# GpSimd's arithmetic in the tiles of an attention and two-layer expert kernel goes to VectorE, its copies of shared halves to ScalarE

## The chip, the cores and the metric

The kernel runs on one core of a Trainium2 chip. That core has a matrix engine (TensorE, in the profile PE, with its weight loads as PEld), three engines for elementwise work (VectorE or DVE, ScalarE or ACT, GpSimd or POOL) and SyncE (SP), which issues most of the DMAs. Each engine works through its own queue in order. The metric is the device time of one execution in microseconds (us), and the time before is the median of three runs. All engines read and write the on-chip SBUF; TensorE writes its results to PSUM, which VectorE and ScalarE read as well.

## The reference

Four steps follow one another, all in float32:

```python
p_packed = sm_attn(p, k, v)            # 8 batches x 8 heads, 32 packed rows over 576 keys
out = sm_attn(q, p_packed, p_packed)   # 576 queries over the 32 packed rows
x = out as (4608, 512)                 # tokens x model
h = x @ w_in                           # 512 -> 2048
g = where(h >= 1, h, where(h <= -1, 0, (h + 1)**2 / 4))
x = g @ w_out                          # 2048 -> 512
# experts: the gate picks one of 8 for each token
logits = x @ w_gate; e = argmax; gate = softmax(logits)[e]
y = gate * (relu(x @ w1[e]) @ w2[e])   # 512 -> 1024 -> 512
```

`sm_attn` is softmax attention with a scale of 1/8. The second attention's softmax runs over 32 columns only.

## The kernel before

**High and low parts.** The matmuls run in a reduced float32 form. A product of two float32 operands is made of three matmuls: high by high, high by low and low by high. So each operand is split: ScalarE rounds it to its high part (a copy into the reduced type), and another engine subtracts that from the original, which gives the low part (names that end in `l`: `al`, `gl`, `xl`).

**Stages.** Packing (to about 102 us by the trace, with some of it going on behind the first tile) makes the first attention, prepares the weights of the first layer, and multiplies them with the packed rows. Then come twelve tiles of tokens with the first two layers. From 820 us on the expert slots follow: 18 of 256 tokens each and a tail of half slots, with the weights of one expert loaded and split for each.

**Tiles.** A pair of batches has 1152 tokens and is cut into three tiles: A (320 columns), M (512) and B (320). B starts where M ends, and A ends where M starts; but the last 64 columns of A make up one block of 128 for the second matmul together with B, so A passes on 256 columns and keeps 64, and B passes on 384. The order of the twelve is M A B, A B M, A B M, M A B. Each tile has 16 steps, one for each 128 of the 2048 hidden columns. In one step `ffn1` makes `h` in PSUM (6 matmuls per batch in the tile, L718), `hidden` makes `g` of it, and `tile_y` adds the step before to `y` in PSUM with three matmuls per block of 128 tokens (L723, L724 with the high part, L725 with the low part).

**`hidden`, the chain of a step.** ScalarE: Relu of 0.5 h + 0.5 (L740) and its square (L741); VectorE: max and min with h (L742), the last reader of `h`; ScalarE: the high part `gh` (L747); then the low part `gl` (L748), on GpSimd in A tiles and on VectorE in M and B tiles. GpSimd also copies A's last 64 columns to `kept` (L750) and, in a B tile, from there to the front of `rt` (L739). `h` has two banks of PSUM, and `gh`, `gl` and `rt` two buffers each.

**Beside it**, in `bg`, steps of other work are laid out by hand for each step: the second attention for the next tile, in chains of three pieces for 256 or 320 columns (`score`, `expo`, `back`; A and B tiles take two chains of 320, M tiles four of 256); the router of the tile before (`gate_items`: eight dot products for each block of 128 tokens, L547, then the places in the expert lists and an indirect DMA by GpSimd, L594); and in the third tile of a pair and the step after it the weights' product with the next packed rows (L361 to L366).

**Order.** SyncE's queue is in the order of the program. For the other engines a planner writes the order: it takes the program's order as priorities and runs through it with costs of its own for each instruction, so a change of engine can change the order of others as well.

Of the kernel before, what the change touches and what calls it, by code (L numbers as in the profile page):

```python
# [15 lines left out]
ALU = mybir.AluOpType  # L16
# [7 lines left out]
P = 128  # L24
TW = 512
HB = 64
# [22 lines left out]
SPLIT = 256  # L49


def tile_kind(t):


    p, m = divmod(t, 3)
    return ("MAB", "ABM", "ABM", "MAB")[p][m]
# [6 lines left out]
def tile_width(t):  # L63
    return TW if tile_kind(t) == "M" else SPLIT + HB
# [13 lines left out]
def tile_blocks(t):  # L78


    return {"A": [0, P], "B": [0, P, 2 * P], "M": [0, P, 2 * P, 3 * P]}[tile_kind(t)]
# [3 lines left out]
def attn_moe_kernel(ctx, tc, qT, kT, vv, pT, wcat, wg, w2cat, out):  # L85
    nc = tc.nc
    ctx.enter_context(tc.manual_schedule(engines={nc.sync.engine}))
    pe, act, dve, pool, sp = nc.tensor, nc.scalar, nc.vector, nc.gpsimd, nc.sync

    def f32(ap):  # L90
        return ap.bitcast(F32)
# [108 lines left out]
    def ps_tile(name):  # L200
        if not done:
            return y_tile(name)
        return a_tile([P, 512], name)
# [25 lines left out]
    def attn_chain(col0, b, ws, n, g, ah, al, pl, sfx):  # L229


        st = {}
        nb = n // 32

        def load():
            qr = pl.tile([P, 2, SPLIT + HB], F32, name="qr" + sfx, tag="qr", bufs=2)
            (act if done else sp).dma_start(qr[:, :, :n], qT[b, 2 * g:2 * g + 2, :, ws:ws + n].rearrange("q p s -> p q s"))
            st["qr"] = qr

            st["sT"], st["aT"] = qr[:, 0, :n].rearrange("p (a r) -> p a r", r=32), qr[:, 1, :n]  # L240

        def score():
            ps = ps_tile("s2" + sfx)
            for q in range(2):
                s = q ^ (b % 2)
                r = slice(D * s, D * s + D)
                pe.matmul(ps[r, :n], lhsT=pkf[:, 2 * g + q, r], rhs=st["qr"][:, q, :n], start=True, stop=True)
            sT = st["sT"]
            dve.transpose(out=sT, in_=ps[:, :n].rearrange("p (a r) -> p a r", r=32))
            mx = pl.tile([P, (SPLIT + HB) // 32, 1], F32, name="mx" + sfx, tag="mx")  # L250
            dve.tensor_reduce(out=mx[:, :nb, 0], in_=sT, axis=AX.X, op=ALU.max)
            pool.tensor_tensor(out=sT, in0=sT, in1=mx[:, :nb, :].to_broadcast([P, nb, 32]), op=ALU.subtract)

        def expo():
            sT = st["sT"]
            act.activation(sT, sT, AF.Exp, scale=SCALE)
            sm = pl.tile([P, (SPLIT + HB) // 32, 1], F32, name="sm" + sfx, tag="sm")
            dve.tensor_reduce(out=sm[:, :nb, 0], in_=sT, axis=AX.X, op=ALU.add)
            dve.tensor_scalar(out=sm[:, :nb, 0], in0=sm[:, :nb, 0], scalar1=1e-9, scalar2=None, op0=ALU.add)
            dve.reciprocal(sm[:, :nb, 0], sm[:, :nb, 0])  # L260
            pool.tensor_tensor(out=sT, in0=sT, in1=sm[:, :nb, :].to_broadcast([P, nb, 32]), op=ALU.mult)

        def back():
            aT = st["aT"]
            hi, lo = ah[:, g, col0:col0 + n], al[:, g, col0:col0 + n]
            dve.transpose(out=aT.rearrange("p (a r) -> p a r", r=32), in_=st["sT"])
            act.copy(hi, aT)
            pool.tensor_tensor(out=lo, in0=aT, in1=f32(hi), op=ALU.subtract)

        return load, [score, expo, back]  # L270

    x_tiles = {}
# [11 lines left out]
    def wtile(n, shape, dt, name):  # L284

        return wpool.tile(shape, dt, name=name, tag=n)
# [440 lines left out]
    kept = []  # L727

    def hidden(t, fc, ps):

        k = tile_kind(t)
        W = tile_width(t)
        gh = work.tile([P, TW], F32R, name=f"gh{FC * t + fc}", tag="gh", bufs=2)
        gl = work.tile([P, TW], F32R, name=f"gl{FC * t + fc}", tag="gl", bufs=2)
        vk = work.tile([P, TW], F32, name=f"rt{FC * t + fc}", tag="rt", bufs=2)
        v, n = vk[:, :W], W
        if k == "B":
            v, n = vk[:, HB:HB + W], HB + W
            pool.tensor_copy(vk[:, :HB], kept[0][:, fc])  # L739
        act.activation(v, ps[:, :W], AF.Relu, bias=half, scale=0.5)  # L740
        act.activation(v, v, AF.Square)  # L741
        dve.scalar_tensor_tensor(out=v, in0=ps[:, :W], scalar=1.0, in1=v, op0=ALU.max, op1=ALU.min)  # L742
        if k == "A":
            n = SPLIT
            if fc == 0:
                kept[:] = [wtile("ws0", [P, FC, HB], F32, f"kept{t}")]
        act.copy(gh[:, :n], vk[:, :n])  # L747
        (pool if k == "A" else dve).tensor_tensor(out=gl[:, :n], in0=vk[:, :n], in1=f32(gh[:, :n]), op=ALU.subtract)  # L748
        if k == "A":
            pool.tensor_copy(kept[0][:, fc], v[:, SPLIT:])  # L750
        return [(gh[:, c:c + P], gl[:, c:c + P]) for c in tile_blocks(t)]

    y_tiles = {}
# [258 lines left out]
    def step():  # L1012
        t, fc = divmod(len(done), FC)
        if fc == 0:
            schedule_tile(t)
        G = t * FC + fc
        ps = h_tile(G, f"h{t}_{fc}")
        ffn1(t, fc, ps)
        gs = hidden(t, fc, ps)
        if done:  # L1020
            tile_y(*done[-1])
        done.append((t, fc, gs))
        for fn in bg.pop(G, []):
            fn()
# [87 lines left out]
```

## Time and profile before

| | |
|---|---|
| median of 3 runs | 1249.33 us (1248.11 to 1250.98) |
| the profiled execution | 1249.28 us, of which the span is 1247.3 |
| TensorE busy | 1193.9 us (96%) |
| its weight loads | 995.3 us (80%) |
| VectorE busy | 944.6 us (76%) |
| ScalarE busy | 730.0 us (59%) |
| GpSimd busy | 325.5 us (26%) |
| mean granted clock of TensorE | 0.984 of full speed |

The span runs from the first instruction to the last one's end. Busy is the time in which an engine runs at least one instruction, and instructions on one engine can overlap at their ends. The ends of matmuls are modelled, so a TensorE that is called busy can still be short of its peak. A wait is idle time of an engine ahead of an instruction, and it is put down to what ended it.

### The profile page before, as it was taken

To read this page: it belongs to the slowest core of one execution; us is meant where nothing else is said; L and a number is where in the kernel's file an instruction comes from. 1 tells how busy PE (TensorE), PEld (TensorE's weight loads), DVE (VectorE), ACT (ScalarE), POOL (GpSimd) and SP (SyncE) were. 2 spreads that over 40 slices of the span, in tenths; PEclk is the share of its full clock that TensorE was granted. 3 is DMA by queue.
4 is the path that set the end of the run, shared out by engine and by line. 5 is a ranking of instruction groups with operands and counts; after the bars stand their busy time and mean duration, and the time that the engine had idled before them with its cause. 6 is when DMAs were issued, how large, how long until landed. Compare 5 with 4: busy or idle time off the path is not lost. (4 is left out here: it accounts for less than half of the span.)

```text
span 1247.3 us, 21251 instructions
## 1 busy us (share of the span) xinstructions
PE 1193.9 (96%) x7234; PEld 995.3 (80%) x7234; DVE 944.6 (76%) x2222; ACT 730.0 (59%) x1430; POOL 325.5 (26%) x567
## 2 busy tenths in 40 slices
PE   5787999999999999999999999999999999999997
PEld 2455888778778887678888887788999999999996
DVE  8888867988895959977869679899766666666663
ACT  4666656667566556565565455655565555555653
POOL 3221116623741105731211265512101000010010
PEclk8988999999999999999999999999999999999999
DMA  9995780143211232111331000601212512111150
GB/s 347 370 328 176 283 245 22 43 142 126 68 47 62 68 113 101 50 44 35 108 126 45 28 18 35 186 18 50 78 36 68 170 44 60 35 54 49 34 178 21
DMA packets 70179, 128.18 MB, mean 103 GB/s; under 512 B 10281, under 2 KB 46633, under 8 KB 66864
## 3 DMA queue, kind: packets, MB, share of 16 engines
q1 hardware_dynamic: 56464, 97.33, 24.2%
q0 software_dynamic: 5840, 18.95, 4.1%
q10 hardware_dynamic: 7760, 10.49, 2.7%
q8 instruction: 59, 0.97, 0.3%
q14 instruction: 56, 0.46, 0.1%
HBM read 162.31 MB, written 31.77 MB: 156 GB/s over the span
## 5 line engine op out<-in xcount | busy, mean ns | idle before, releaser
L718 PE MATMUL h<-ah,pw 128*128 128x256 f32 (+1 forms) x1024 | 242.6, 302 | 8.2 <-DVE rt L742 8.0
L869 DVE TENSOR_TENSOR sw<-raw,sw 128x1024 fp32r<-128x1024 f32 (+1 forms) x152 | 180.9, 1209 | 77.9 <-ACT sw L867 77.8
L885 PEld LDWEIGHTS gh<-gx,sw 128*128 128x128 f32 x1728 | 227.1, 191 | 12.8
L885 PE MATMUL gh<-gx,sw 128*128 128x256 f32 x1728 | 230.5, 283 | 0.0
L723 PE MATMUL y<-wo,gh 128*128 128x512 f32 x576 | 229.9, 399 | 0.6 <-ACT kp L423 0.6
L724 PE MATMUL y<-wo,gh 128*128 128x512 f32 x576 | 228.5, 397 | 0.0
L547 DVE CUSTOM_DVE_ANT_0 jk<-yr,wgb 128x512 bf16<-128x512 f32 x288 | 219.1, 761 | 5.6 <-ACT yr L775 3.5
L718 PEld LDWEIGHTS h<-ah,pw 128*128 128x128 f32 x1024 | 176.5, 190 | 31.0 <-DVE rt L742 13.4
L867 ACT CAST sw<-raw 128x1024 fp32r<-128x1024 f32 (+1 forms) x160 | 156.5, 1004 | 59.1 <-PE gy L725 53.9
L725 PE MATMUL y<-wo,gl 128*128 128x512 f32 x576 | 186.3, 400 | 2.1 <-POOL gl L748 1.9
L740 ACT ACTIVATE rt<-h,half 128x320 f32<-128x320 f32 (+1 forms) x192 | 111.0, 580 | 102.6 <-PE h L718 86.2
L747 ACT CAST gh<-rt 128x512 fp32r<-128x512 f32 (+2 forms) x192 | 98.1, 512 | 96.6 <-DVE rt L742 59.1
L718 PE MATMUL h<-al,pw 128*128 128x256 f32 (+1 forms) x512 | 152.7, 298 | 0.0
L742 DVE SCALAR_TENSOR_TENSOR rt<-h,rt 128x320 f32<-128x320 f32 (+1 forms) x192 | 105.5, 551 | 51.1 <-ACT rt L741 46.3
L908 POOL DMA_INDIRECT out<-go,xm x37 | 36.8, 993 | 362.3 <-ACT go L907 303.1
L725 PEld LDWEIGHTS y<-wo,gl 128*128 128x128 f32 x576 | 105.8, 189 | 30.0 <-POOL gl L748 5.1
L723 PEld LDWEIGHTS y<-wo,gh 128*128 128x128 f32 x576 | 108.7, 189 | 23.3 <-issue 2.1
L724 PEld LDWEIGHTS y<-wo,gh 128*128 128x128 f32 x576 | 108.9, 189 | 18.7
L889 ACT ACTIVATE ggh<-gh 128x256 fp32r<-128x256 f32 x144 | 55.0, 382 | 109.5 <-PE gh L885 103.8
L724 PE MATMUL gy<-sw,ggh 128*128 128x512 f32 x288 | 113.9, 395 | 0.0
L723 PE MATMUL gy<-sw,ggh 128*128 128x512 f32 x288 | 113.8, 395 | 0.0
L748 DVE TENSOR_TENSOR gl<-rt,gh 128x512 fp32r<-128x512 f32 (+1 forms) x128 | 84.1, 658 | 25.3 <-ACT gh L747 21.2
(220 smaller groups left out, 1762.5 us busy)
## 6 DMA issues: line engine op xcount, KB each, us to landing
raw<-in_w2cat SPq DMA_DIRECT2D x76, 1024.0 KB
ws<-wsd SPq DMA_DIRECT2D x48, 512.0 KB
wr<-in_wcat SPq DMA_DIRECT2D x16, 1024.0 KB
kp<-in_kT SPq DMA_DIRECT2D x16, 576.0 KB
xb<-xs SPq DMA_DIRECT2D x72, 128.0 KB
vr<-in_vv SPq DMA_DIRECT2D x16, 512.0 KB
wsd<-ws SPq DMA_DIRECT2D x8, 1024.0 KB
qr<-in_qT ACTq DMA_DIRECT2D x16, 320.0 KB
```

Of the source, the lines that this page charges most:

```text
L547: dve.tensor_tensor_reduce(out=junk, in0=rows[j][:, :DM], in1=wgb[0][:, e, :], scale=1.0, scalar=0.0, op0=ALU.mult, op1=ALU.add, accum_out ...
L718: pe.matmul(ps[:, col0:col0 + n], lhsT=w[:, g, part, c], rhs=x[:, g, col0:col0 + n], start=(n_mm == 0), stop=(n_mm == 5))
L723: pe.matmul(y, lhsT=gh, rhs=wh, start=first, stop=False)
L724: pe.matmul(y, lhsT=gh, rhs=wl, start=False, stop=False)
L725: pe.matmul(y, lhsT=gl, rhs=wh, start=False, stop=last)
L740: act.activation(v, ps[:, :W], AF.Relu, bias=half, scale=0.5)
L742: dve.scalar_tensor_tensor(out=v, in0=ps[:, :W], scalar=1.0, in1=v, op0=ALU.max, op1=ALU.min)
L747: act.copy(gh[:, :n], vk[:, :n])
L748: (pool if k == "A" else dve).tensor_tensor(out=gl[:, :n], in0=vk[:, :n], in1=f32(gh[:, :n]), op=ALU.subtract)
L867: act.copy(w[:, n, 0], r)
L869: (pool if sid == 0 and i else dve).tensor_tensor(out=w[:, n, 1], in0=r, in1=f32(w[:, n, 0]), op=ALU.subtract)
L885: pe.matmul(ps[:, :SL], lhsT=first(sid, 4 * (fc // 4) + k, part)[:, c], rhs=rh[:, k, :], start=(n_mm == 0), stop=(n_mm == 3 * KD - 1))
```

## The change

Six instructions get another engine; operands, sizes and places in the program stay. The subtraction of the maximum and the multiplication with the reciprocal sum in the second attention, and the low part of its result, go from GpSimd to VectorE, in all tiles. So does the low part of `hidden` in A tiles, which makes all tiles alike. The two copies of 64 columns (`kept`) go from GpSimd to ScalarE. On GpSimd stay the indirect DMAs, the router's running counts (L571 to L573), copies of token numbers (L593), copies in the packing (L395), and eight low parts of the first slot's weights (L869).

```diff
 def attn_chain / score:
-    pool.tensor_tensor(out=sT, in0=sT, in1=mx[:, :nb, :].to_broadcast([P, nb, 32]), op=ALU.subtract)
+    dve.tensor_tensor(out=sT, in0=sT, in1=mx[:, :nb, :].to_broadcast([P, nb, 32]), op=ALU.subtract)
 expo:
-    pool.tensor_tensor(out=sT, in0=sT, in1=sm[:, :nb, :].to_broadcast([P, nb, 32]), op=ALU.mult)
+    dve.tensor_tensor(out=sT, in0=sT, in1=sm[:, :nb, :].to_broadcast([P, nb, 32]), op=ALU.mult)
 back:
-    pool.tensor_tensor(out=lo, in0=aT, in1=f32(hi), op=ALU.subtract)
+    dve.tensor_tensor(out=lo, in0=aT, in1=f32(hi), op=ALU.subtract)
 def hidden:
     if k == "B":
-        pool.tensor_copy(vk[:, :HB], kept[0][:, fc])
+        act.copy(vk[:, :HB], kept[0][:, fc])
...
     act.copy(gh[:, :n], vk[:, :n])
-    (pool if k == "A" else dve).tensor_tensor(out=gl[:, :n], in0=vk[:, :n], in1=f32(gh[:, :n]), op=ALU.subtract)
+    dve.tensor_tensor(out=gl[:, :n], in0=vk[:, :n], in1=f32(gh[:, :n]), op=ALU.subtract)
     if k == "A":
-        pool.tensor_copy(kept[0][:, fc], v[:, SPLIT:])
+        act.copy(kept[0][:, fc], v[:, SPLIT:])
```

## Rows read from the trace of the kernel before

**Rows 1.** Busy us by stage: length, then PE, PEld, DVE, ACT, POOL, clock, DMA share, GB/s.

```profile
40.00:102.10 62.10, 47.45 (x472) 28.14 (x476) 52.02 (x101) 37.35 (x92) 16.05 (x26) 0.84 0.98 348
...
191.10:235.20 44.10, 43.82 (x228) 35.18 (x227) 39.62 (x126) 27.58 (x77) 31.94 (x46) 1.00 0.09 28
235.20:290.80 55.60, 54.99 (x276) 45.55 (x275) 47.61 (x124) 39.68 (x92) 16.42 (x34) 1.00 0.41 133
290.80:341.00 50.20, 48.80 (x245) 38.19 (x244) 42.28 (x122) 30.20 (x70) 32.01 (x50) 1.00 0.23 77
...
468.80:516.20 47.40, 45.98 (x233) 36.25 (x232) 44.97 (x118) 29.67 (x69) 31.28 (x47) 1.00 0.23 79
...
721.00:764.00 43.00, 41.37 (x211) 33.91 (x210) 37.40 (x106) 24.35 (x57) 28.87 (x44) 1.00 0.05 19
...
820.20:1247.30 427.10, 419.56 (x2634) 376.86 (x2632) 284.64 (x512) 234.04 (x350) 41.81 (x44) 1.00 0.22 64
```

**Rows 2.** Waits of TensorE, 191 to 820 us: total us, times, longest.

```profile
PE h L718 <- DVE rt L742: 8.0, 9, 2.0
PE y L725 <- POOL gl L748: 1.9, 4, 1.1
...
PEld h L718 <- DVE rt L742: 13.2, 15, 2.3
PEld y L725 <- POOL gl L748: 5.1, 7, 1.5
```

**Rows 3.** The dots by line in four A tiles, then an M tile: busy us, mean ns.

```profile
L547 DVE CUSTOM_DVE_ANT_0 jk<-yr,wgb 128x512 bf16<-128x512 f32 x32 | 25.0, 780 | 1.5 <-ACT yr L775 1.1
...
L547 DVE CUSTOM_DVE_ANT_0 jk<-yr,wgb 128x512 bf16<-128x512 f32 x24 | 19.6, 817 | 0.2
...
L547 DVE CUSTOM_DVE_ANT_0 jk<-yr,wgb 128x512 bf16<-128x512 f32 x29 | 26.5, 915 | 0.1
...
L547 DVE CUSTOM_DVE_ANT_0 jk<-yr,wgb 128x512 bf16<-128x512 f32 x32 | 26.8, 839 | 2.5 <-ACT yr L775 2.3
...
L547 DVE CUSTOM_DVE_ANT_0 jk<-yr,wgb 128x512 bf16<-128x512 f32 x24 | 16.3, 681 | 0.4 <-ACT yr L775 0.2
```

**Rows 4.** Timeline in two A tiles: start us, us, instruction, count.

```profile
200.23 0.88 DVE L742 SCALAR_TENSOR_TENSOR rt<-h,rt 128x320 f32<-128x320 f32 x2
...
483.36 1.25 DVE L547 CUSTOM_DVE_ANT_0 jk<-yr,wgb 128x512 bf16<-128x512 f32 x1
...
482.80 2.42 POOL L748 TENSOR_TENSOR gl<-rt,gh 128x256 fp32r<-128x256 f32 x2
```

**Rows 5.** GpSimd by line over the span: busy us, mean ns, idle before.

```profile
L748 POOL TENSOR_TENSOR gl<-rt,gh 128x256 fp32r<-128x256 f32 x64 | 59.6, 932 | 12.2 <-ACT gh L747 4.9 <-PE y L725 4.7 <-DMA qr<-in_qT 1.3
...
L750 POOL COPY kept<-rt 128x64 f32<-128x64 f32 x64 | 32.2, 503 | 42.6 <-DVE rt L742 39.7 <-PE h L718 2.5
L268 POOL TENSOR_TENSOR al<-qr,ah 128x256 fp32r<-128x256 f32 (+1 forms) x32 | 31.8, 993 | 41.1 <-ACT ah L267 41.0
L252 POOL TENSOR_TENSOR qr<-qr,mx 128x256 f32<-128x256 f32 (+1 forms) x32 | 26.0, 812 | 132.8 <-issue 52.4 <-DVE mx L251 45.9 <-PE h L718 33.5
L261 POOL TENSOR_TENSOR qr<-qr,sm 128x256 f32<-128x256 f32 (+1 forms) x32 | 25.9, 808 | 35.2 <-DVE sm L260 26.4 <-DVE rs L424 3.6 <-ACT rt L741 2.9
L739 POOL COPY rt<-kept 128x64 f32<-128x64 f32 x64 | 23.8, 375 | 68.5 <-DVE gl L748 67.5 <-DVE pk L219 0.5 <-issue 0.2
```

**Rows 6.** VectorE by line and shape over the span.

```profile
L742 DVE SCALAR_TENSOR_TENSOR rt<-h,rt 128x320 f32<-128x320 f32 x128 | 61.7, 484 | 17.2 <-ACT rt L741 15.6 <-POOL yr L593 0.4
L890 DVE SCALAR_TENSOR_TENSOR ggl<-gh,ggh 128x256 fp32r<-128x256 f32 x144 | 59.9, 416 | 49.5 <-ACT ggh L889 47.0 <-PE y L725 2.4
```

**Rows 7.** Waits of ScalarE and VectorE, 191 to 820 us.

```profile
ACT rt L740 <- POOL gl L748: 7.5, 10, 2.4
...
DVE gl L748 <- ACT gh L747: 15.8, 26, 1.9
```

**Rows 8.** ScalarE by line and shape over the span.

```profile
L218 ACT CAST pk<-bt 64x64 fp32r<-64x64 f32 x64 | 13.1, 205 | 2.5 <-PE bt L209 1.8
```

## The prediction

> **What bounds the kernel now.** I read the busy times by stage first, one stage for each of the twelve tiles. A tile's stretch runs from its first Relu (L740) to the next tile's. From 820 us on, the expert slots run with TensorE busy 419.6 of 427.1 us, and no line that the change touches runs there [rows 1]. The gain or loss has to arise before 820 us. There, the B tile at 235 us has TensorE busy 55.0 of 55.6 us. The four A tiles (191, 291, 469 and 721 us) stand out for something else: GpSimd is busy 29 to 32 us of 43 to 50, against 16 in that B tile and 16 in the last 62 us of the packing. VectorE is busy 39.62 + 42.28 + 44.97 + 37.40 = 164.3 of their 184.7 us, 89%, so 20.4 us idle in all [rows 1]. In A tiles two engines are nearly full, TensorE and VectorE, and a third one, GpSimd, stands in the chain of each step.
>
> Next the waits of TensorE between 191 and 820 us [rows 2]. The matmul array and its weight loads are two engines of the profile, and one stall can show on either or on both. Two things alone hold them: L718 waits for L742 (the step before last has to be read out of PSUM before its bank is used again), 8.0 us on the one and 13.2 on the other; and L725, the only matmul that needs the low part, waits for GpSimd's L748, 1.9 and 5.1 us. No wait of L725 for a low part made on VectorE comes near these, although VectorE makes it in eight of the twelve tiles. So the low part from GpSimd costs up to 1.9 + 5.1 = 7.0 us of TensorE, and a late L742 13.2 (if the two columns are the same stalls) to 21.2.
>
> Then why L742 is late. It stands in VectorE's queue between the router's dot products (L547). In an M tile with GpSimd busy little, a dot takes 681 ns; in the four A tiles 780, 817, 915 and 839 ns [rows 3]. The timeline of the A tile at 469 us shows a dot of 1.25 us beside two GpSimd subtractions that together take 2.42 us [rows 4], where one takes 932 ns on average [rows 5]. Both engines lengthen each other.
>
> The Trainium skill, "SBUF — State Buffer", section "Who interferes with whom", says that a VectorE instruction with two SBUF inputs and a GpSimd instruction that reads SBUF exclude each other for the whole instruction. The rows on the dots agree. By that rule the whole lengthening of the dots goes and the load that the A tiles gain on VectorE is the +12.4 us worked out below; if the dots were long for another reason, it would be +30.7.
>
> **The change part by part.** The profiled execution took 1249.28 us (span 1247.3 and 2.0 around it), 0.05 under the median of 1249.33; I work from 1249.3.
>
> *The price of a moved pass.* VectorE doesn't show these passes with 256 and 320 columns from SBUF. The nearest rows are L742 at 128x320, 484 ns, and L890 at 128x256, 416 ns [rows 6]; both read one input from PSUM. Two L742 in a row take 0.88 us, not 0.97 [rows 4], so the second starts 0.40 us after the first: a full queue pays some 0.08 us less than the duration. I take 0.40 and 0.33 us; the bounds are 0.33 (all as the smaller) and 0.484 (full duration).
>
> *Low parts in A tiles.* 64 x 0.33 = 21.1 us on VectorE, 5.3 in each A tile, against 59.6 us freed on GpSimd [rows 5].
>
> *The attention's passes.* 32 chains with three passes each, 96 in all [rows 5]. An M tile has four chains of 256 columns, an A or B tile two of 320, so 48 x 0.40 + 48 x 0.33 = 35.0 us. The four chains of tile 0 run in the packing: 12 x 0.33 = 4.0 us beside a VectorE busy 52.0 of 62.1 us. There the DMA share is 0.98 [rows 1], which covers most of it. Bounds: 0, or all 4.0 us on the path if the cover is gone; I take 1. In each A tile run two chains for the B tile after it: 4 x 6 x 0.40 = 9.6 us.
>
> *Relief.* The dots lose 32 x 0.099 + 24 x 0.136 + 29 x 0.234 + 32 x 0.158 = 3.2 + 3.3 + 6.8 + 5.1 = 18.3 us in the A tiles, if they fall to 681 ns [rows 3].
>
> *VectorE in the A tiles, the sum.* +21.1 + 9.6 - 18.3 = +12.4 us, against 20.4 us idle: 176.7 of 184.7, 96%. It still fits, hardly. A fuller queue makes L742 wait more behind others; no tile of before stands at 96% over its whole length with VectorE alone to blame. The nearest is the A tile at 469 us, 95% busy: there TensorE is idle 47.4 - 46.0 = 1.4 us, in the one at 721 us, 87% busy, 43.0 - 41.4 = 1.6 us [rows 1]. From those two a fuller VectorE costs nothing measurable. Bounds: 0, and +12.4 if none of the idle time can be used; I take +3, a quarter, nearer to those rows.
>
> *A wait that comes along.* On VectorE the low part stands behind the cast L747 of ScalarE, in order; behind it stand the dots and the next L742. Where VectorE makes it now (128 times) that wait is 15.8 us between 191 and 820 us [rows 7]. At the same 0.12 us, 64 more would add 7.9 us of idle VectorE, part of the bound just given.
>
> *TensorE's two stalls.* The waits for GpSimd's low part go: bounds 0 (VectorE just as late) and -7.0; I take -5, since low parts made on VectorE show no such stall. Of the 13.2 to 21.2 us behind L742, the part caused by long dots should go; bounds 0 and -21.2, and I take -3, about a quarter of the smaller figure, because the load on the queue stays.
>
> *Copies to ScalarE.* 64 + 64 copies of 64 columns, 503 and 375 ns on GpSimd [rows 5]. ScalarE's nearest row is a cast of 64x64, 205 ns [rows 8]: 16 x 0.21 = 3.4 us per A or B tile, on a ScalarE busy 24 to 40 of 43 to 56 us [rows 1]. The copy out of a tile follows the cast, the copy into the next one precedes it; each delays what stands behind it on ScalarE (the next Relu, then L742) by up to 0.21 us. On the other side, L740 loses its wait for GpSimd's L748, 7.5 us [rows 7]. Bounds: -7.5 and 128 x 0.205 = +26 if nothing covered them, which the idle share of ScalarE excludes for most; I take +0.5.
>
> *Nothing moves* among the DMAs: GpSimd keeps its indirect writes, its counting adds and the eight L869 of the first slot, and stands ready earlier for them.
>
> Sum: -5 - 3 + 3 + 1 + 0.5 = -3.5 us, 1249.3 - 3.5 = 1245.8, so **1246**.
>
> **The rivals.**
> 1. *The forecast, 1241 to 1247 us, chance 0.36.* For it: the length of the dots, the L725 stalls. Against: VectorE at 96%.
> 2. *One wait for another, about 1249 us, chance 0.26.* TensorE stays the bound everywhere, and the low part is as late from a full VectorE as it was from GpSimd: 0 for the stalls, +0.5 to +1.5 for the rest. For it: TensorE is idle only 0.28 + 1.40 + 1.42 + 1.63 = 4.7 us in the A tiles by its busy times [rows 1].
> 3. *VectorE becomes the bound of the A tiles, slower, about 1260 us, chance 0.26.* Its idle time there is waiting for ScalarE, and it stays: the A tiles grow by the net load, 12.4 us, less some 2 of the stalls, so 1249.3 + 10.4 = 1259.7. If the dots stayed long as well, it would be 30.7 - 20.4 = 10.3 us even with no idle left. It decides where VectorE's idle time in the A tiles doesn't fall from 20.4 below about 8 us. The Trainium skill speaks for this one: "Perfetto Trace Analysis", section "Optimizing Scalar/DVE Operations", says that work may be moved to ScalarE or even GpSimd when VectorE is saturated, and the change goes the other way; the same section warns that between VectorE and GpSimd the move may not help.
> 4. *Both stalls go almost entirely, about 1235 us, chance 0.12.* The most is 7.0 + 21.2 = 28.2 us; half of it gives 1249.3 - 14.1 = 1235.2.
>
> The order of instructions on each engine is written anew by the planner for the new costs, which no row of before shows; it can shift any of these by a few us, and with cases 2 and 3 it sets the chances.
>
> **Range and chances.** A measurement of this kernel tells about 0.2%, 2.5 us, from no change. Cases 1 and 4 give faster, less a little of case 1 that ends within 2.5 us: 0.46. Case 2 with that edge: 0.26. Case 3 and the edge of case 2: 0.28. The range from 1234 to 1259.5 leaves out half of case 4 and about half of case 3. For case 1 alone it is 1241 to 1247.
>
> **What would show it.** Dots in A tiles near 681 ns (relief), no wait of L725 above 1 us in all (low part), VectorE busy about 177 us in the four A tiles whatever their length, the A tiles together no longer than 185 us, ScalarE 3 to 4 us busier in each, the slots from the first to the last unchanged at 427 us. Wrong if L718's wait for L742 grows past 21 us, if the A tiles together pass 192 us, or if the packing grows by more than 2 us.

## The result, and the profile after

The changed kernel takes 1256.8 us (median of 6 runs, 1254.05 to 1258.59), against 1248.72 us (6 runs, 1247.52 to 1250.98) for the kernel before: ratio 1.006 [1.0049, 1.0071], 8 us slower where 3.5 us faster was forecast. The profiled execution took 1256.77 us, its span is 1255.0, and its mean granted clock 0.978.

Busy times by engine, first part of the page of the changed kernel:

```profile
PE 1197.9 (95%) x7234; PEld 1001.4 (80%) x7234; DVE 965.2 (77%) x2382; ACT 748.7 (60%) x1558; POOL 135.1 (11%) x279
```

GpSimd fell by 190 us, VectorE grew by only 20.6 although it took over 160 instructions of 0.41 us or more, and ScalarE by 18.7. TensorE has 4.0 us more busy time for the same 7234 instructions.

The stages of the changed kernel, tiles 0 to 3, 6, 10 and 11 and the slots; columns as in [rows 1]:

```profile
99.90:193.10 93.20, 87.95 (x610) 71.72 (x610) 67.10 (x110) 54.55 (x94) 0.18 (x1) 0.96 0.65 221
193.10:234.00 40.90, 40.90 (x217) 34.47 (x216) 35.47 (x117) 28.69 (x85) 3.02 (x4) 1.00 0.08 23
234.00:305.10 71.10, 66.02 (x314) 52.72 (x312) 59.42 (x171) 45.89 (x117) 8.42 (x17) 0.96 0.33 105
305.10:351.40 46.30, 42.88 (x209) 33.78 (x209) 42.72 (x139) 31.23 (x85) 3.47 (x7) 0.92 0.26 87
...
482.30:525.00 42.70, 42.50 (x220) 34.82 (x222) 41.48 (x127) 32.05 (x85) 2.26 (x4) 1.00 0.23 81
...
727.10:767.50 40.40, 40.40 (x212) 34.52 (x212) 35.05 (x117) 26.84 (x72) 4.24 (x6) 1.00 0.04 14
767.50:828.90 61.40, 57.10 (x289) 47.98 (x288) 51.06 (x160) 38.61 (x91) 20.18 (x22) 0.97 0.38 112
828.90:1255.00 426.10, 416.87 (x2617) 374.49 (x2615) 283.38 (x509) 232.19 (x346) 42.42 (x44) 1.00 0.22 64
```

The four A tiles, which were to show the gain or to become the bound, are all shorter: 40.9 + 46.3 + 42.7 + 40.4 = 170.3 us against 184.7 [rows 1]. That is no gain by itself. They hold 217 + 209 + 220 + 212 = 858 matmul instructions where they held 228 + 245 + 233 + 211 = 917; work has moved over their edges. An estimate: at 184.7 / 917 = 0.20 us each, these 59 alone are 11.9 of the 14.4 us. Tiles 2 and 3 together have nearly the same count as before (523, was 521), and they grew from 55.6 + 50.2 = 105.8 to 117.4 us. TensorE idles in them (66.02 of 71.10 and 42.88 of 46.30 us busy), and they are the only tiles whose clock was 1.00 before [rows 1] and falls now (0.96, 0.92).

Tile lengths of the two profiled executions, from each tile's first Relu (L740) to the next's, sum up the difference. Tile 11 and the slots stand in one row: the borders between them that are used above (828.9) and in [rows 1] (820.2) lie at different points of the program, one behind the first matmul of a slot's `gy` and one ahead of it.

| stage | before | after | difference |
|---|---|---|---|
| up to tile 0 | 102.1 | 99.9 | -2.2 |
| tile 0 (M) | 89.0 | 93.2 | +4.2 |
| tile 1 (A) | 44.1 | 40.9 | -3.2 |
| tiles 2 (B) and 3 (A) | 105.8 | 117.4 | +11.6 |
| tiles 4 to 10 | 423.0 | 416.1 | -6.9 |
| tile 11 (B) and all behind it | 483.3 | 487.5 | +4.2 |
| span | 1247.3 | 1255.0 | +7.7 |

Waits of TensorE from 193 to 829 us in the changed kernel, columns as in [rows 2]:

```profile
PEld pp L361 <- issue: 8.7, 7, 3.0
...
PE pp L361 <- DMA ws<-wsd: 5.7, 5, 2.6
...
PEld h L718 <- DVE rt L742: 4.7, 4, 2.8
...
PEld y L725 <- DVE gl L748: 3.0, 6, 0.9
PE h L718 <- DVE rt L742: 3.0, 2, 2.3
...
PE y L725 <- DVE gl L748: 0.7, 2, 0.5
```

Both stalls of [rows 2] shrank: L742 from 8.0 and 13.2 to 3.0 and 4.7, the low part from 1.9 and 5.1 to 0.7 and 3.0. The new wait is L361, the weights' product with the next packed rows, which waits for a DMA ("issue" is idle time for which the profile shows nothing that was waited for).

That DMA is `reload`: SyncE brings 512 KB of split weights for each product into one of two halves of a buffer, and the next reload into that half waits for the product that reads it. Sixteen products stand in `bg`, one in each step from the fifth of tile 2 on. Before, TensorE waited for such a reload for 0.6 us in tiles 2 and 3 (its weight loads for 1.0). The timeline of TensorE in the changed kernel (start, us, instruction, in brackets the wait ahead of it; most lines between are left out):

```profile
227.18 0.18 PE L576 MATMUL rk<-M,utri 128*128 128x16 f16 x1
...
230.57 0.44 PE L209 MATMUL bt<-ident,packed 128*64 128x128 f32 x4
...
239.78 0.44 PE L209 MATMUL bt<-ident,packed 128*64 128x128 f32 x4
...
251.37 0.86 PE L361 MATMUL pp<-ws,pk 128*128 128x512 f32 x3
252.07 0.18 PE L576 MATMUL rk<-M,utri 128*128 128x16 f16 x1
...
257.09 0.44 PE L209 MATMUL bt<-ident,packed 128*64 128x128 f32 x4
...
267.66 0.86 PE L361 MATMUL pp<-ws,pk 128*128 128x512 f32 x3
...
292.18 0.86 PE L361 MATMUL pp<-ws,pk 128*128 128x512 f32 x3
294.60 0.95 PE L361 MATMUL pp<-ws,pk 128*128 128x512 f32 x3 [0.86 <-DMA ws<-wsd]
298.18 0.94 PE L361 MATMUL pp<-ws,pk 128*128 128x512 f32 x3 [2.63 <-DMA ws<-wsd]
300.44 1.62 PE L361 MATMUL pp<-ws,pk 128*128 128x512 f32 x3 [1.32 <-DMA ws<-wsd]
302.86 1.62 PE L361 MATMUL pp<-ws,pk 128*128 128x512 f32 x3 [0.27 <-DMA ws<-wsd]
306.11 1.62 PE L361 MATMUL pp<-ws,pk 128*128 128x512 f32 x3 [0.57 <-DMA ws<-wsd]
```

and the same instructions in the kernel before:

```profile
218.32 0.18 PE L576 MATMUL rk<-M,utri 128*128 128x16 f16 x1
...
222.29 0.44 PE L209 MATMUL bt<-ident,packed 128*64 128x128 f32 x4
...
231.99 0.44 PE L209 MATMUL bt<-ident,packed 128*64 128x128 f32 x4
...
237.56 0.19 PE L576 MATMUL rk<-M,utri 128*128 128x16 f16 x1
...
239.64 0.86 PE L361 MATMUL pp<-ws,pk 128*128 128x512 f32 x3
...
242.24 0.44 PE L209 MATMUL bt<-ident,packed 128*64 128x128 f32 x4
...
253.75 0.85 PE L361 MATMUL pp<-ws,pk 128*128 128x512 f32 x3
```

L576 is the router's matmul, which needs the dots of the tile before; L209 builds the next packed rows, which the products need. The two groups of L576 come 8.9 and 14.5 us later, of which 2.0 are the later start of tile 1; the builds come 8.3, 7.8 and 14.9 us later, the first product 11.7 and the second 13.9. The products then crowd: six in a row start 2 to 4 us apart, five of them with a wait for their reload. From the eighth product (292.18) to the eleventh (300.44) no matmul of `h` stands between them in the changed kernel; in the kernel before, between three and four steps of `h` stand there. In stretches of 8 us (columns as in [rows 1]):

```profile
288.00:296.00 8.00, 6.69 (x30) 4.34 (x29) 6.62 (x16) 4.71 (x9) 1.34 (x4) 1.00 0.73 179
296.00:304.00 8.00, 4.23 (x11) 2.95 (x12) 6.78 (x15) 3.33 (x7) 0.41 (x1) 0.69 0.51 182
304.00:312.00 8.00, 6.04 (x18) 4.49 (x17) 7.39 (x18) 5.50 (x14) 0.00 (x0) 0.50 0.64 217
312.00:320.00 8.00, 8.00 (x40) 6.23 (x39) 6.16 (x17) 5.20 (x13) 0.00 (x0) 0.95 0.17 61
```

TensorE idles for 1.31 and 3.77 us in the first two stretches; its granted clock goes to 0.50, the 1.2 GHz level, and three matmuls take 1.62 us in place of 0.86. The Trainium skill, "TensorE: Matmul & The Clock Gate", section "HAM oscillation — how this bites in real kernels", describes a kernel in which the wait for the next slice of an operand from a DMA drops the clock, so that the work behind the wait is paid at half speed; these rows agree. An estimate: 5.7 us of waits, and of the busy time above 4.23 x 0.31 + 6.04 x 0.50 + 8.00 x 0.05 = 4.7 us lost to the clock, 10.4 together, against the 11.6 us that tiles 2 and 3 grew.

Why the router is late: the dots by line in the changed kernel's four A tiles and, last, in B tile 2:

```profile
L547 DVE CUSTOM_DVE_ANT_0 jk<-yr,wgb 128x512 bf16<-128x512 f32 x25 | 17.1, 682 | 0.1
...
L547 DVE CUSTOM_DVE_ANT_0 jk<-yr,wgb 128x512 bf16<-128x512 f32 x18 | 12.1, 672 | 0.1
...
L547 DVE CUSTOM_DVE_ANT_0 jk<-yr,wgb 128x512 bf16<-128x512 f32 x24 | 16.4, 684 | 0.3 <-ACT yr L775 0.3
...
L547 DVE CUSTOM_DVE_ANT_0 jk<-yr,wgb 128x512 bf16<-128x512 f32 x29 | 19.8, 684 | 0.8 <-ACT yr L775 0.7
...
L547 DVE CUSTOM_DVE_ANT_0 jk<-yr,wgb 128x512 bf16<-128x512 f32 x29 | 19.7, 680 | 0.2
```

and in B tile 2 of the kernel before:

```profile
L547 DVE CUSTOM_DVE_ANT_0 jk<-yr,wgb 128x512 bf16<-128x512 f32 x16 | 11.7, 729 | 0.2
```

Each dot is as fast as forecast (672 to 684 ns, was 780 to 915 [rows 3]), but tile 1 holds 25 of them, not 32, and B tile 2 holds 29, where the kernel before had 16. VectorE does the new low parts first, and the dots slide into the tile behind.

The moved instructions, VectorE by line and shape:

```profile
L748 DVE TENSOR_TENSOR gl<-rt,gh 128x256 fp32r<-128x256 f32 x64 | 26.0, 414 | 5.7 <-PE y L725 4.4 <-ACT gh L747 1.0
...
L252 DVE TENSOR_TENSOR qr<-qr,mx 128x320 f32<-128x320 f32 x16 | 7.7, 481 | 0.0
```

On ScalarE the copies L750 and L739 take 243 and 240 ns, 15.4 us each for 64.

### The profile page after: what moved, and what is told of

It is laid out like the page before. It is cut to its first block, busy times and chain, and to the rows that moved or that the text cites. A ratio compares the mean times of both kernels' runs of the same rounds, so it can differ in the third digit from the quotient of the medians.

```text
span 1255.0 us, 21146 instructions
## 1 busy us (share of the span) xinstructions
PE 1197.9 (95%) x7234; PEld 1001.4 (80%) x7234; DVE 965.2 (77%) x2382; ACT 748.7 (60%) x1558; POOL 135.1 (11%) x279
## 4 chain that ended last, share of the span: by engine, by line
PE 84%; DVE 4%; DMA 2%; ACT 1%; issue 1%; POOL 0%; POOLq 0%; ACTq 0%; DVEq 0%
PE gh L885 16%; PE h L718 16%; PE y L723 10%; PE y L725 10%; PE y L724 10%; PE gy L725 5%; PE gy L723 5%; PE gy L724 5%; PE pp L361 3%; PE s L247 1%; PE pp L348 1%; DMA ws<-wsd 1%; DVE sw L869 1%; DVE pw L366 1%; DVE jk L547 1%
## 5 line engine op out<-in xcount | busy, mean ns | idle before, releaser
L718 PE MATMUL h<-ah,pw 128*128 128x256 f32 (+1 forms) x1024 | 244.4, 303 | 6.1 <-DVE rt L742 3.2
L869 DVE TENSOR_TENSOR sw<-raw,sw 128x1024 fp32r<-128x1024 f32 (+1 forms) x152 | 182.3, 1217 | 76.1 <-ACT sw L867 75.8
L547 DVE CUSTOM_DVE_ANT_0 jk<-yr,wgb 128x512 bf16<-128x512 f32 x288 | 196.2, 681 | 5.4 <-ACT yr L775 4.2
L718 PEld LDWEIGHTS h<-ah,pw 128*128 128x128 f32 x1024 | 178.3, 192 | 24.3 <-issue 5.9
L725 PE MATMUL y<-wo,gl 128*128 128x512 f32 x576 | 183.3, 398 | 0.7 <-DVE gl L748 0.7
L740 ACT ACTIVATE rt<-h,half 128x320 f32<-128x320 f32 (+1 forms) x192 | 111.1, 581 | 121.8 <-PE h L718 107.9
L718 PE MATMUL h<-al,pw 128*128 128x256 f32 (+1 forms) x512 | 153.2, 299 | 0.2
L742 DVE SCALAR_TENSOR_TENSOR rt<-h,rt 128x320 f32<-128x320 f32 (+1 forms) x192 | 105.4, 551 | 47.3 <-ACT rt L741 41.5
L747 ACT CAST gh<-rt 128x512 fp32r<-128x512 f32 (+2 forms) x192 | 98.1, 511 | 63.1 <-DVE rt L742 40.9
L748 DVE TENSOR_TENSOR gl<-rt,gh 128x512 fp32r<-128x512 f32 (+2 forms) x192 | 107.0, 560 | 27.6 <-ACT gh L747 17.6
L725 PEld LDWEIGHTS y<-wo,gl 128*128 128x128 f32 x576 | 105.0, 188 | 26.3 <-DVE gl L748 3.0
L889 ACT ACTIVATE ggh<-gh 128x256 fp32r<-128x256 f32 x144 | 55.0, 382 | 109.8 <-PE gh L885 100.5
L718 PEld LDWEIGHTS h<-al,pw 128*128 128x128 f32 x512 | 98.0, 191 | 7.7 <-DVE al L268 0.6
```

What stands on the lines that cost most here:

```text
L547: dve.tensor_tensor_reduce(out=junk, in0=rows[j][:, :DM], in1=wgb[0][:, e, :], scale=1.0, scalar=0.0, op0=ALU.mult, op1=ALU.add, accum_out ...
L718: pe.matmul(ps[:, col0:col0 + n], lhsT=w[:, g, part, c], rhs=x[:, g, col0:col0 + n], start=(n_mm == 0), stop=(n_mm == 5))
L725: pe.matmul(y, lhsT=gl, rhs=wh, start=False, stop=last)
L748: dve.tensor_tensor(out=gl[:, :n], in0=vk[:, :n], in1=f32(gh[:, :n]), op=ALU.subtract)
L869: (pool if sid == 0 and i else dve).tensor_tensor(out=w[:, n, 1], in0=r, in1=f32(w[:, n, 0]), op=ALU.subtract)
```

## The experiments

Two theories stood against each other. Theory 1, order: the low parts in tile 1 push the router's dots of tile 0 back, and with them the products, which then wait for their reloads while the clock falls. Theory 2, load: VectorE simply has more to do, wherever that is, and this sets the time. Each kernel was timed together with the kernel before (1248.85 to 1249.0 us in the three sessions); ratios are to that.

**One part at a time.** The low part alone, on the kernel before:

```diff
-    (pool if k == "A" else dve).tensor_tensor(out=gl[:, :n], ...)
+    dve.tensor_tensor(out=gl[:, :n], ...)
```

> The kernel before with one part of the change: the low part of A tiles on VectorE; attention passes and copies stay on GpSimd. Theory 1 (order): the A tiles gain some 10 us as they did with the whole change, the products of the next pair's weights stand later and closer in TensorE's queue (first one with its operands at step 8 of the B tile, 10 in the changed kernel, 6 before), so the B tile at 235 us and the A tile behind it lose part of that again: 1244 to 1248 us. Theory 2 (load): VectorE's load alone sets the loss, 21 of the 56 us moved: 1251 us.

Measured: 1251.57 us (1248.29 to 1252.41), ratio 1.0016 [1.0006, 1.0026]. Theory 1's number was missed: the part alone costs 2.7 us, which is within 0.6 of Theory 2's 1251. TensorE waits 3.4 us for reloads in its profiled execution, which took 1249.06 us, 2.5 below its median, and kept the clock at 1.00; its tiles 2 and 3 took 105.5 us, as long as before. So that profile does not show where the 2.7 us went, and this run doesn't tell the theories apart.

The three passes of the attention alone (`pool` to `dve` at L252, L261 and L268):

> The kernel before with one part of the change: the three passes of the second attention on VectorE; low parts of A tiles and copies stay on GpSimd. Theory 1 (order): the products keep their place in TensorE's queue (step 6), so no wait for reloads; the rest is small: 1247 to 1251 us. Theory 2 (load): 35 of the 56 us moved onto VectorE with the dots still lengthened by GpSimd: 1253 to 1256 us.

Measured: 1248.75 us (1246.48 to 1250.75), ratio 0.9999 [0.999, 1.0009]. No wait for reloads in tiles 2 and 3. Theory 1's range was met, and Theory 2 (1253 to 1256) is refuted for this part: 96 more passes on VectorE cost nothing in all.

The two copies alone (`pool.tensor_copy` to `act.copy` at L739 and L750):

> The kernel before with one part of the change: the two copies of 64 columns on ScalarE. Theory 1: the order of the products stays, fewer GpSimd instructions lengthen the dots: 1244 to 1249 us. Theory 2: VectorE's load is the same, so 1248 to 1250 us.

Measured: 1247.49 us (1246.23 to 1250.72), ratio 0.9992 [0.9982, 1.0001]. Theory 1's range was met, Theory 2's missed by 0.5 us, which is too little to tell them apart.

Low part and copies together, that is the change without the attention's passes:

> The changed kernel with the three passes of the second attention back on GpSimd. Theory 1: A tiles as short as in the changed kernel, products at step 8 and less close: 1243 to 1248 us. Theory 2: load between e1 and before: 1249 to 1252 us.

Measured: 1252.15 us (1249.53 to 1252.88), ratio 1.0021 [1.0011, 1.0031]. TensorE waits 1.8 us for a reload, and its clock is 0.61 from 296 to 304 us. Theory 1's number was missed again; Theory 2's 1249 to 1252 was met but for 0.15. Taken alone the three parts make 2.7 - 0.1 - 1.4 = +1.2 us; the whole makes +8. So the parts don't add. That speaks against load alone.

**Take the collision away.** On the changed kernel, and as a control on the kernel before, reloads bring 64 of 512 columns, except the first two of each pair; the rest of the weights is left out, and later products use what lies in the buffer:

```diff
-        sp.dma_start(f32(ws1[0][:, k % 2]), wsd[2 * n + k // 2, :, k % 2])
+        w = 512 if n == 0 and k < 2 else 64
+        sp.dma_start(f32(ws1[0][:, k % 2, :, :w]), wsd[2 * n + k // 2, :, k % 2, :, :w])
```

> The changed kernel, but each reload of the second layer-one weight halves brings 64 of 512 columns (64 KB for 512 KB); the first two of a pair stay whole. It leaves out the rest of the reload, so the later products use stale weights; every instruction on TensorE, VectorE, ScalarE and GpSimd stays. Theory 1 (TensorE waits for reloads behind products that stand too close, and its clock falls in that stall): no such wait, granted clock 1.00 between 230 and 350 us, the B tile at 235 us and the A tile behind it together some 106 to 109 us, not 117: 1244 to 1249 us. Theory 2 (VectorE's load): as the changed kernel, 1254 to 1258 us.

> The kernel before with the same short reloads (it leaves out the same part), as a control. Theory 1: before shows only 1.6 us of TensorE waiting for reloads, so 1245 to 1249 us. If it gains as much as the changed kernel does from short reloads, reloads aren't what tells the two kernels apart. Theory 2: 1247 to 1250 us.

Measured: 1250.02 us (1247.19 to 1253.08), ratio 1.0001 [0.9988, 1.0013], for the changed kernel; 1250.71 us (1249.22 to 1253.57), ratio 1.001 [1.0001, 1.002], for the control. Tiles 2 and 3 of the changed kernel with short reloads:

```profile
235.40:299.60 64.20, 62.98 (x311) 50.95 (x310) 55.61 (x163) 45.34 (x116) 9.59 (x17) 1.00 0.12 37
299.60:343.50 43.90, 41.22 (x208) 32.20 (x209) 43.02 (x130) 31.00 (x83) 3.24 (x6) 1.00 0.21 62
```

The products stand at nearly the same steps as in the changed kernel and VectorE has the same work, yet TensorE waits for no reload, the clock stays at 1.00 and the two tiles take 108.1 us in place of 117.4. The control's take 104.8 us, so 3.3 of the 11.6 us stay. With short reloads the two kernels are level (-0.7 us, where it was +8), though the changed one ends 1 us above Theory 1's range. The control is 1.7 us slower than the kernel before, above both its ranges, for a reason not found. So the loss goes with the full reloads; Theory 2 is refuted for it.

**Spread the products.** On the changed kernel, products and reloads a step and a half apart:

```diff
-                at(base + 4 + i, lambda n=n, k=k: product(p + 1, n, k))
+                at(base + 4 + i * 3 // 2, lambda n=n, k=k: product(p + 1, n, k))
...
-                    at(base + 4 + i, lambda n=n1, k=k1: reload(p + 1, n, k))
+                    at(base + 4 + i * 3 // 2, lambda n=n1, k=k1: reload(p + 1, n, k))
```

> The changed kernel with the products laid out one and a half steps apart (not one). The first products keep their place, the last eight spread from two steps of the A tile over thirteen. Theory 1: the reloads get time, the stall and the fall of the clock shrink: 1246 to 1252 us. Theory 2: nothing is taken off VectorE: 1254 to 1258 us.

Measured: 1258.99 us (1258.04 to 1259.87), ratio 1.0078 [1.0061, 1.0095]. Theory 1's expectation was wrong, and Theory 2's 1254 to 1258 was missed by 1. Waits for reloads fell to 3.2 us and tiles 2 and 3 to 113.7, but the products of the next pair now run into A tile 6, and tiles 5 to 7 take 181.4 us in place of 173.0 (932 matmul instructions for 928). So spreading the products is no remedy; what makes those tiles longer is not shown.

**Where the low part counts.** All low parts on VectorE except in tiles 1 and 3, the copies on ScalarE, the attention on GpSimd as before:

```diff
+    (pool if t in (1, 3) else dve).tensor_tensor(out=gl[:, :n], ...)
```

> The copies on ScalarE, the low part on VectorE only in the third and fourth A tile (469 and 721 us), the attention passes on GpSimd. Theory 1: the order around the first products stays that of before (first product with its operands at step 5 of the B tile), the two A tiles get shorter by some 7 us together, part of it given back behind them: 1241 to 1246 us. Theory 2: more load on VectorE than in the run with the copies alone: 1248 to 1251 us.

Measured: 1246.64 us (1244.46 to 1247.34), ratio 0.9975 [0.9965, 0.9984]. This beats both kernels, by 2.3 us (of medians) against the kernel before in that session, and lies below Theory 2's 1248 to 1251; Theory 1's 1241 to 1246 was overrun by 0.6.

The next two are the changed kernel in full, with the 16 low parts of one A tile back on GpSimd: of tile 1, and of tile 3.

```diff
-    dve.tensor_tensor(out=gl[:, :n], ...)
+    (pool if t == 1 else dve).tensor_tensor(out=gl[:, :n], ...)
```

> The changed kernel with the low parts of one A tile, the first (191 us), back on GpSimd: 16 instructions. Theory 1: the router's dots of that tile come sooner, and the first products stand at step 6 of the B tile as before (10 in the changed kernel): no stall on reloads, clock 1.00, tiles 3 and 4 together some 103 to 107 us: 1246 to 1250 us. Theory 2 (VectorE's load counts wherever it lies): 5.3 of 56 us less, 1255 to 1257 us.

> The same with the second A tile (at 305 us in the changed kernel) in place of the first: 16 instructions, as much VectorE time. Theory 1: the first products stay at step 10 and close together, so the stall stays: 1254 to 1260 us. Theory 2: as the run before, 1255 to 1257 us; a gain as large as that run's would speak against theory 1.

Measured: 1250.26 us (1248.31 to 1253.01), ratio 1.0009 [0.9997, 1.002], with tile 1 on GpSimd; 1260.47 us (1258.04 to 1261.81), ratio 1.009 [1.007, 1.011], with tile 3. The same instructions and nearly the same VectorE time (966.2 and 963.7 us busy), 10 us apart. Against the changed kernel's 1256.8 us (timed apart; the kernel before differs by 0.3 us), the 16 low parts of tile 1 cost 6.5 us on VectorE, and those of tile 3 gain 3.7 there. Tiles 2 and 3, the second group of the route's matmuls and the first products, tile 1 on GpSimd:

```profile
239.40:294.50 55.10, 54.97 (x274) 45.23 (x273) 48.56 (x140) 41.80 (x108) 8.79 (x16) 1.00 0.38 125
294.50:341.60 47.10, 46.11 (x233) 36.20 (x232) 43.37 (x127) 33.51 (x86) 2.44 (x4) 1.00 0.25 82
```

```profile
242.64 0.17 PE L576 MATMUL rk<-M,utri 128*128 128x16 f16 x1
...
248.28 0.86 PE L361 MATMUL pp<-ws,pk 128*128 128x512 f32 x3
...
257.90 0.85 PE L361 MATMUL pp<-ws,pk 128*128 128x512 f32 x3
```

and tile 3 on GpSimd:

```profile
234.50:306.20 71.70, 66.52 (x314) 52.89 (x312) 59.44 (x172) 45.91 (x118) 8.46 (x17) 0.95 0.34 105
306.20:352.10 45.90, 43.70 (x211) 34.52 (x210) 39.79 (x125) 30.28 (x85) 17.32 (x24) 0.89 0.27 87
```

```profile
251.85 0.86 PE L361 MATMUL pp<-ws,pk 128*128 128x512 f32 x3
...
268.14 0.86 PE L361 MATMUL pp<-ws,pk 128*128 128x512 f32 x3
```

With tile 1 on GpSimd, B tile 2 holds 17 dots, the first products come earlier, and TensorE keeps its clock; with tile 3, it holds 29 dots, and the loss is whole. Part of the 15.4 us between their tiles 2 and 3 is count: 507 matmul instructions against 525, some 3.6 us at 0.20 each. With tile 3 on GpSimd TensorE also waits 3.5 us for reloads behind tile 3, and its clock is 0.96 in tile 6. Theory 1's ranges were overrun by 0.3 and 0.5 us; Theory 2's 1255 to 1257 was missed by 5 below and by 3.5 above.

Last, the kernel before with the copies on ScalarE and the low parts of tiles 3, 6 and 10 on VectorE:

> Copies on ScalarE, attention passes on GpSimd, low parts on VectorE in all A tiles but the first. Theory 1: the products' places of before, and the second A tile has its low parts on VectorE too: 1243 to 1247 us, no slower than the run with the first two A tiles on GpSimd. Theory 2: more load on VectorE than that run, 1247 to 1249 us.

Measured: 1246.86 us (1245.89 to 1249.02), ratio 0.9988 [0.9978, 0.9998]. Theory 1's range was met; Theory 2's 1247 to 1249 was missed by 0.1. So the low parts of tile 3 do no harm either.

**All together.** Where the second product stands among TensorE's steps (tile_step, counted from 0, of the last whole step of `h` ahead of it in the trace), beside the profiled executions. The step that the expectations give for the "first product" is that of this second one; the first stands behind 2_2 in the kernel before and behind 2_5 in the changed one, and doesn't tell the kernels apart (behind 2_3 both with the attention alone and with low parts and copies).

| kernel | second product | TensorE's wait for reloads, tiles 2 and 3 | tiles 2 and 3 | median |
|---|---|---|---|---|
| before | 2_6 | 0.6 | 105.8 | 1249 |
| attention alone | 2_6 | none | 101.1 | 1248.75 |
| copies alone | 2_5 | 0.6 | 103.6 | 1247.49 |
| copies, low parts of 6, 10 | 2_5 | 0.7 | 103.3 | 1246.64 |
| copies, low parts of 3, 6, 10 | 2_5 | 0.7 | 103.3 | 1246.86 |
| after, tile 1 on GpSimd | 2_6 | none | 102.2 | 1250.26 |
| low parts alone | 2_8 | 3.4 | 105.5 | 1251.57 |
| low parts and copies | 2_8 | 1.8 | 110.3 | 1252.15 |
| after | 2_10 | 5.7 | 117.4 | 1256.8 |
| after, tile 3 on GpSimd | 2_10 | 6.5 | 117.6 | 1260.47 |

Each kernel of the table with the low parts of tile 1 on VectorE has its second product behind step 8 or later and a wait of 1.8 us or more; each one without has it behind step 5 or 6 and a wait of at most 0.7.

## Why the prediction was wrong, point by point

**Right.** Dots near 681 ns: 672 to 684. The prices on VectorE: durations of 0.414 and 0.481 us, as in the nearest rows (0.416 and 0.484), and the 0.08 us taken off for overlap was about right: summed by line, VectorE's instructions take 37.7 us more, its busy time, which counts an overlap once, 20.6 more, so an estimate is 17.1 us for 160 instructions, 0.11 each. ScalarE paid 0.24 against 0.21. L742's stalls: by 5.0 on the matmuls and 8.5 on the weight loads, more than the 3 us taken. The slots, from the first slot's Relu (L889): 430.6 us for 430.3. The dots' lengthening goes as a whole: between 193 and 830 us 272 of them took 208.1 us before, mean 765 ns, and 268 take 182.6 after, mean 681. The rule cited from the Trainium skill ("SBUF — State Buffer", section "Who interferes with whom") agrees with these rows, in that the dots are short once GpSimd is quiet; whether one engine waits out the other's whole instruction, no run here shows.

**Mis-sized.** The low part's stalls were taken to go by 5 of 7.0 us; 0.7 + 3.0 stay, so 3.3 went. The mark "no wait of L725 above 1 us in all" failed by the weight loads. ScalarE is busier in the four A tiles by 118.8 - 111.8 = 7.0 us, 1.8 in each, not 3 to 4; over the span its 128 copies add 18.7. The packing with tile 0 ends 2.0 us later, where 1 was taken. Tile 11 and all behind it had no term of their own and take 4.2 us more.

**The step that failed** is "A fuller queue makes L742 wait more behind others", with its +3 between 0 and +12.4. The queue is fuller, but L742 isn't what waits: its stalls shrank. What has the lowest priority waits, the router's dots; VectorE's busy time in the A tiles is 154.7 us, not 176.7; 21 of 117 dots left them, which is 14.3 of these 22.0 us at 0.68 each. Behind the late dots stand, by the order of the traces, the route, and behind it the builds and the products that fetch their weights through two half buffers. The prediction asked what is late next on VectorE for the low part and L742 only. "Nothing moves among the DMAs" put at nothing, without a look at the reloads, what became 5.7 us of waits, and the sum has no term for the clock that falls behind them. Its sentence that the planner's order "can shift any of these by a few us" named the place, and left it unpriced; tiles 2 and 3 grew by 11.6 us. None of its three signs of being wrong came up (L718's wait 3.0 and 4.7 us, the A tiles 170.3, the packing 99.9): the loss began in B tile 2, which none of them watched.

**The rivals.** Rival 3 had the direction and nearly the time (about 1260), but not the mechanism: A tiles are shorter, and VectorE's load in tile 3 does not carry the loss, which is as large without the low parts there. Its sign, that VectorE's idle time in the A tiles stays above 8 us, came up (170.3 - 154.7 = 15.6), but because dots had left, not because the tiles grew. That its time was near is luck. The rule cited with it (the Trainium skill, "Perfetto Trace Analysis", section "Optimizing Scalar/DVE Operations": relieve a saturated VectorE) holds here for one tile alone: the 16 low parts of tile 1 are better on GpSimd, those of tiles 3, 6 and 10 no worse on VectorE. Rival 2's level result is what the change gives without the collision (short reloads: -0.7 us). So the forecast's -3.5 would have failed even then: against the control, tile 0 takes 93.3 us for 89.6, and tile 11 with all behind it 487.8 for 483.7.

**Shown and not shown.** Shown: the loss hangs on the 16 low parts of tile 1, and goes when the reloads are short. Read from trace and order, but not tried by itself: the link from the late dots to the late products. The route's result, the builds of the next packed rows and the products take their banks in turn from the same three of PSUM, the memory that all matmuls of this kernel write to (none writes to SBUF), so a late route would hold up what follows in the rotation. The timelines fit: a build (L209) follows the route's two groups by 3.4 and 5.0 us (before 4.0 and 4.7), the first product comes behind the second build after the first group, and the second product behind the build after the second group. The first product doesn't wait for the second group itself: in the changed kernel it starts 0.7 us ahead of it. A kernel with banks of its own for the route wasn't made. How much of the 11.6 us is wait and how much clock stays an estimate. A third buffer for the reloads wasn't tried. What lengthens tile 0 and the stretch from tile 11 on is open; the attention's passes alone do it as well (92.2 and 487.5 us) without a loss in all, the copies alone don't (89.6 and 483.6), and the two fastest kernels take 488.6 from tile 11 on. That the change with tile 1 on GpSimd ends 3.4 us above the version without the attention's passes (1246.86) is open too.

## What to carry to other kernels

When an engine gets more work, look for what in its queue has the lowest priority, and follow that to what an in-order TensorE meets next; here the loss lay behind late background dots, not in the chain that gained. Move work by place: 16 subtractions on VectorE cost 6.5 us in one tile and gain 3.7 in another, and the version with only the copies and the late low parts moved is the fastest (1246.64 us, ratio 0.9975 [0.9965, 0.9984]), though not told apart from the one with tile 3's as well (1246.86). Compare stretches by their count of matmuls, not by their names: the A tiles got 14.4 us shorter in a kernel that got slower.

## What was not expected of the hardware

In the changed kernel TensorE idled for 1.31 and 3.77 us in two stretches of 8, and the clock was 0.69 in the second and 0.50 and 0.95 in the next two. With short reloads 2.95 us of idle time in one such stretch (296 to 304 us) left it at 1.00, and in the low parts alone 3.4 us of waits did too, while low parts and copies together had 0.61 beside a wait of 1.8 us. So idle time of this size can cost once, or again through the clock. And VectorE took over 26.0 us of low parts and 43.2 us of attention passes and grew by 20.6 us only: the same 288 dots gave back 22.9 (219.1 to 196.2 us), other instructions that got shorter 8.6, and 17.1 went into overlap.
